# SBUF tiles in four pools by their role on TensorE, and a new plan for the same instructions

## The chip, the cores and the metric

One core of a Trainium2 chip runs the whole kernel. The metric is the device time of one execution in microseconds (us); lower is better. The profile names the engines PE (TensorE matmuls), PEld (TensorE weight loads, which overlap the matmuls), DVE (VectorE), ACT (ScalarE), POOL (GpSimd) and SP (the queue that starts nearly all DMAs).

## The reference

Attention by random features on 8 batches x 8 heads x 576 tokens x 64 columns, followed by a gated block on the 4608 x 512 result. All of it is float32.

```python
proj = einsum('bhsd,md->bhsm', x, omega); h = proj - sum(x*x)/2; phi = exp(h - max(h)) / sqrt(m)
kv = einsum('bhsm,bhsd->bhmd', k_p, v);  z = sum(k_p, axis=2)
attn = einsum('bhsm,bhmd->bhsd', q_p, kv) / (einsum('bhsm,bhm->bhs', q_p, z)[..., None] + 1e-06)
x = attn.transpose(0, 2, 1, 3).reshape(4608, 512)
out = ((x @ w_a) * (x @ w_b)) @ w_out          # 512 -> 1536 -> 512
```

## The kernel before

**Two kinds of work on PE.** The attention part consists of short float32 matmuls in bursts: projections (`four`, L633), the product of k features and v (`kv_burst`, L910), and the numerator (`num`, L982 and L985). The gated block consists of long matmuls in the rounded float32 type. Each float32 operand is split into a high and a low part, and a product is the sum of three matmuls (high-high, high-low, low-high). Of tokens there are 8 main blocks of 512 (b = 0 to 7), and one tail block (b = 8) that is made up of the last 64 tokens of each batch.

**The gated block.** `moe_block` (b = 0, 1) makes a and b with matmuls of 512 columns (L1319: stationary tile `w` or `u`, moving tile `x`, `Sa` or `Sb`) and multiplies the product with w_out by matmuls of 512 columns (`Out.mm`, L1129: stationary `ghl`, moving `wo`, three matmuls at a time). `moe_block7` (b = 2 to 8) uses a scheme with seven half-size products in place of eight. Its function `product` (L1405, matmuls at L1410) issues six matmuls of 256 columns, two moving tiles times three high-low combinations. One `unit` has seven products and one unit is one step; a main block has 12 steps. The stationary tile of a product is a slice of `w`, of `t` (reloaded from DRAM in every unit) or of `bq`; the moving tile is `x`, `Sa` or `Sb`. The products with w_out are again L1129 for b = 2 to 6, and for b = 7 and 8 a seven-product scheme at L1198 (stationary `ghl` or `og`, moving `wo` or `ot`). The results are added up from PSUM by DVE (L1420 and others).

**SBUF.** Every tile belongs to a ring of slots (L397 to L400); a slot is one tag in a tile pool, as large as its largest tile. Some tiles are guests in the slots of other rings (`IN_U` at L402, `LATE` at L405). For example `t` lives in u2 to u6, `bq` in a0 and a1, `xa` (first half of two of the four x tiles of a block) in xa0, xa1, u10 or u11, `ot` in X0, X1, hq1 and qd0, `og` in nat0, nat1, ht0 and ht1, and late `wo` tiles in hk0 and hq0 besides their own three slots. Constants come first and end at byte 1088 of each partition. Then one pool `sp` holds all other slots (L387, `alloc` at L409), which lie one behind another in the order in which the program first uses them. Slots for matmul operands are multiples of 512 bytes; between them lie small ones: `sm` with 192 bytes, `sq` with 64, `dn` with 36, `rd` with 20 (starts are rounded up to 32 bytes). So the starts of large tiles fall on all multiples of 32 modulo 256. In the built program, for example, both slots of `Sb` start at 128 modulo 256 (bytes 126848 and 164224), and the five slots in which `t` lives start at 160, 128, 128, 0 and 192 modulo 256 (bytes 25248, 156032, 160128, 181248, 204992). Below, the distance of a matmul is the byte address of its moving operand less that of its stationary operand, modulo 256. Slices within a tile start at multiples of 512 bytes, so the distance is the same for all slices.

**The plan.** All work is first written down as a graph of operations (class `Graph`). `schedule` then plays it through with a cost for each operation, a due time from `dues`, and a shift or tilt from the tables `SHIFT` and `TILT` (by number of the operation). That settles the order on each engine, whether a copy goes to ACT or to DVE, and which slot each tile gets. `PLACE` says at which step of the gated block the burst of each head pair u is put. In the last rows of the table, `CFG["XL"]` gives the steps of block 7 from which the tail block's x may be loaded (`xl`, first number) and split into high and low parts and sums (second number; L1525, L1526, `split` and `sums` with L424, L432 and L589). `CFG["LOWP"]` names raw weight pieces whose low part POOL extracts.

Of the kernel before, what the change touches and what calls it, by code (L numbers as in the profile page):

```python
# [15 lines left out]
X = mybir.AxisListType.X  # L16
# [3 lines left out]
B, H, S, D, M = 8, 8, 576, 64, 128  # L20
# [16 lines left out]
EPS = 1e-6 * M  # L37
KS = NHP

CFG = dict(TWIN=(0, 1, 2, 3, 4, 6, 7), LOWP=(1, 6, 10, 12, 13, 16, 19, 20, 21, 22, 25, 33, 34), SQP=('natk_0_0', 'natk_0_1', 'natq_0_0', 'natq_0_1', 'natq_0_3'), BW=365.0, DLAT=(1500, 2600), QUEUE=8, XL=(0, 2), JOIN=(6, 7, 8, 9, 10), LOWD=430, SQB=1, GLUE=700, TURNS=99, EDF=("DVE", "ACT", "POOL"), ROUNDS=1, SQUEEZE=1, CAP=("DVE", "ACT", "POOL"), ZS=600, ZB=(1500, 3000, 5000), ZD=(1500, 3000, 4500), HQ=(2500, 4000, 5000), BACK2=(1500, 2500, 4000), TW=(), WAIT=0, RAW=2000, FAST=(0, 1, 2, 3), JOIN0=False, WARM=8, HROOM=["w0", "u1", "w1", "u2", "w2", "u3"], H=3, TURN=(7,), BACK=1500, AT=2, MERGED=(5, 12, 13, 14, 15, 16, 17, 18, 19, 20, 21, 22, 23, 24, 25, 26, 27, 28, 29, 30, 31), SQPE=4, MARGIN=1200, LOAD=2500, SUMS=1400, NATS=(2,), CONV=(22000, 2200))  # L40


PLACE = {4: 3, 5: 4, 6: 7, 7: 9, 8: 10, 9: 12, 10: 14, 11: 18, 12: 20, 13: 21, 14: 27, 15: 29, 16: 33, 17: 35, 18: 38, 19: 41, 20: 45, 21: 47, 22: 50, 23: 54,
         24: 58, 25: 59, 26: 62, 27: 66, 28: 67, 29: 70, 30: 74, 31: 77, 32: 78, 33: 83}


SHIFT = {49: -8000, 89: 1500, 99: -4000, 123: 500, 156: -4000, 179: -1000, 253: 9500, 459: -1000, 558: -2000, 629: 500, 633: -500, 646: -4000, 730: 8000, 749:
         8000, 989: 4500, 995: -8000, 1081: 4000, 1200: 8000, 1207: 4000, 1339: 4000, 1352: 5000, 1483: -8000, 1546: 8000, 1587: 3000, 1957: -8000, 2016:
         1500, 2248: -2000, 2395: -8000, 2854: 3500, 3508: -4000, 3860: -2000, 3940: 6000, 4192: 2000}
TILT = {15: 800, 19: -800, 21: 800, 30: 3000, 34: -800, 58: 3000, 75: -3000, 79: 800, 81: 800, 88: -3000, 105: 800, 109: -800, 115: -3000, 124: 3000, 135:  # L50
# [9 lines left out]


class Buf:
# [7 lines left out]
    def part(self, k):  # L70
        return self, k
# [26 lines left out]
class Graph:  # L98
# [79 lines left out]
    def dues(self):  # L178
# [16 lines left out]
        for o in self.order:  # L195
            if "PE" in o.eng:
                idle += max(0, o.start - at - 5) * CFG["SQUEEZE"]
                at = o.end
# [11 lines left out]
        while heap:  # L210
            d, _, o = heapq.heappop(heap)
            e = next(iter(o.eng))
            cost = o.end - o.start if o.bytes else o.eng[e]
            if e in CFG["CAP"]:
                now = min(-d, ptr.get(e, inf))
# [12 lines left out]
    def plan(self):  # L228

        self.schedule()  # L230
        for _ in range(CFG["ROUNDS"]):
            self.dues()
            self.schedule()
        for o in self.ops:
            o.shift, o.tilt = SHIFT.get(o.n, 0), TILT.get(o.n, 0)
        self.schedule()
# [9 lines left out]
    def schedule(self):  # L246
# [12 lines left out]
        def entry(o, x, t):  # L259

            t = max(t, free[x] + 112 * (x == "DVE" and o.port == twice == 2))
            if x == "DVE" and o.port and port["POOL"][0] < t:
                t = max(t, port["POOL"][1] - 135)
            elif x == "POOL" and port["DVE"][0] <= t:
                t = max(t, port["DVE"][1] - 140)
            return t
# [20 lines left out]
        while len(done) < len(self.ops):  # L287
            best = None
            for e in engines:
                mine = None  # L290
                for o in ready[e]:
# [3 lines left out]
                    s = entry(o, e, max(o.need, at[0] + 92 * (e == "PE" and at[0] > 0)))  # L295
                    if o.bytes and len(landed) >= CFG["QUEUE"]:
                        s = max(s, landed[-CFG["QUEUE"]] + 100)
                    for x in o.eng:
# [3 lines left out]
                    else:  # L302


                        wait = CFG["WAIT"] if e == "DVE" and 0 <= o.prio < 4000 else 0
                        pr = o.shift + (o.prio if o.due is None or e not in CFG["EDF"] else o.due)
# [76 lines left out]
def tile_attention_moe(ctx: ExitStack, tc: tile.TileContext, kqt, kqtt, kqn, kqnt, vx, omst, idn, wab, wout, out):  # L383
    nc = tc.nc
    SQPE = CFG["SQPE"]
    const = ctx.enter_context(tc.tile_pool(name="const", bufs=1))
    sp = ctx.enter_context(tc.tile_pool(name="sp", bufs=1))  # L387
    ps = ctx.enter_context(tc.tile_pool(name="ps", bufs=1, space=PSUM))
    dram = ctx.enter_context(tc.tile_pool(name="dram", bufs=1, space=bass.MemoryType.DRAM))
    wide = wab.dtype == I64  # L390
# [6 lines left out]
    for name, n in dict(X=2, Xw=0, nat=2, x2=0, v=1, xg=1, hk=1, hq=3, qd=1, kvz=0, sm=3, sq=3, ht=3, Xt=1, xl=0, xts=2, rd=2, x=4, xa=2, xf=2, Sa=2, Sb=2, st=0,  # L397
                        w=NF // 2, rw=0, u=NF, t=0, tst=0, wo=3, raw=2, a=2, c=0, bq=0, ghl=2, osb=0, ot=0, owr=0, og=0, ogf=0, oc=0, zs=1, z2=1, zb=2, k2=4, dn=1, tails=0, zq=2, zx=2,
# [7 lines left out]
                oc=["v0", "xg0", "Xt0", "raw0", "raw1"])  # L406
    PS = {"at", "ab", "o"}

    def alloc(b):  # L409
        pool = ps if b.ring in PS else sp  # L410
        b.ap = pool.tile(b.shape, b.dtype, tag=b.slot, name=b.name)

    def fixed(shape, dtype, name):
# [27 lines left out]
    for k in range(4):  # L441
        g.op({"POOL": 110}, lambda e, k=k: nc.gpsimd.memset(ind.ap[D * (k // 2):D * (k // 2) + D, D * (k % 2):D * (k % 2) + D], SQ2 * (k in (0, 3))),
             w=[(ind, k)], alloc=[ind] if k == 0 else [], prio=-5000)
# [55 lines left out]
    for kind, i, ws in units:  # L499
        n = place[kind, i, ws[0]]  # L500
# [1005 lines left out]
    def bursts(step, place, banks):  # L1506

        for u, at in PLACE.items():
            if at == step:
# [25 lines left out]
    with tc.manual_schedule():  # L1535
        for o in order:
            for b in o.alloc:
                alloc(b)
            o.fn(next(iter(o.eng)))
# [74 lines left out]
```

## Time and profile before

| | us |
|---|---|
| median of three runs | 1033.49 (1033.02 to 1034.39) |
| profiled execution | 1033.61 |
| its span in the trace | 1031.8 |
| first matmul, last matmul's end (from the span's start) | 1.0, 1026.9 |

The profiled execution is 0.1 us above the median, and 1.8 us of its time lie outside of the span. "Busy" of an engine is the time in which at least one of its instructions runs. Matmuls are pipelined: one of 256 columns is listed with some 281 ns, but the next one starts some 118 ns after it. So what a stream of matmuls costs is read from the distance of starts, not from durations.

### The profile page before, as it was taken

The numbers are of one execution on the slowest core, as the hardware profiler recorded it, in microseconds if no ns is written. First come the engines' busy times: TensorE is split into PE (matmuls) and PEld (weight loads), VectorE is DVE, ScalarE is ACT, GpSimd is POOL, SyncE is SP. The second block draws the span as 40 slices with busy tenths as digits, with TensorE's granted clock in tenths as the row PEclk, the third lists the DMA queues.
The fourth block names the chain that finished last, engine by engine and source line by source line (L and its number), as shares of the span: only waits on it lengthen the run. The fifth ranks groups of instructions, "written<-read, shape, count | busy, mean of one in ns | idle before, by whom it ended". The sixth has DMA issues, their size and how long they took to land.

```text
span 1031.8 us, 27457 instructions
## 1 busy us (share of the span) xinstructions
PE 1021.0 (99%) x10538; PEld 902.8 (87%) x10538; DVE 876.7 (85%) x2162; ACT 575.5 (56%) x1584; POOL 109.1 (11%) x157
## 2 busy tenths in 40 slices
PE   9999999999999999999999999999999999999998
PEld 7777777777798989989998988988998999999998
DVE  6999999899997979877996889888877578999776
ACT  7998897667755647655663566475454024232221
POOL 0221222101111111111110111111110000000000
PEclk9999999999999999999999999999999999999999
DMA  9778877998899988999899989988887889999991
GB/s 353 292 254 258 283 247 244 309 327 303 297 318 375 323 293 296 339 307 298 276 314 339 301 272 321 334 261 299 280 297 251 279 297 332 307 348 334 366 322 43
DMA packets 123428, 306.76 MB, mean 297 GB/s; under 512 B 17952, under 2 KB 41248, under 8 KB 123296
## 3 DMA queue, kind: packets, MB, share of 16 engines
q1 hardware_dynamic: 122416, 304.34, 86.1%
q8 instruction: 83, 1.36, 0.5%
q10 hardware_dynamic: 880, 0.66, 0.2%
q14 instruction: 49, 0.40, 0.1%
HBM read 249.60 MB, written 55.34 MB: 296 GB/s over the span
## 4 chain that ended last, share of the span: by engine, by line
PE 91%; DVE 6%; ACT 2%; issue 1%; DVEq 0%; ACTq 0%
PE p L1410 40%; PE o L1129 23%; PE pb L1319 5%; PE pa L1319 5%; PE o_P L1198 5%; PE pkv L910 3%; PE ppk L633 3%; PE p L633 2%; PE p L982 2%; DVE sm L659 1%; DVE raw L482 1%; PE p L1198 1%; PE ppq L633 1%; PE pm L982 1%; ACT hk L672 0%
## 5 line engine op out<-in xcount | busy, mean ns | idle before, releaser
L1420 DVE TENSOR_TENSOR c<-p,c 128x512 f32<-128x512 f32 (+1 forms) x336 | 208.6, 621 | 72.1 <-PE p L1410 68.4
L1129 PE MATMUL o<-wo,ghl 128*128 128x512 f32 x1008 | 258.3, 397 | 0.0
L1129 PEld LDWEIGHTS o<-wo,ghl 128*128 128x128 f32 x1008 | 181.4, 188 | 39.7 <-issue 5.0
L1410 PE MATMUL p<-x,w 128*128 128x256 f32 x1008 | 136.5, 281 | 0.2
L1410 PEld LDWEIGHTS p<-x,w 128*128 128x128 f32 x1008 | 131.0, 188 | 6.5 <-DVE c L1420 0.6
L1410 PE MATMUL p<-Sa,t 128*128 128x256 f32 x1008 | 133.1, 281 | 0.0
L1410 PEld LDWEIGHTS p<-Sa,t 128*128 128x128 f32 x1008 | 125.5, 188 | 0.1
L424 ACT COPY c<-p 128x256 f32<-128x256 f32 x84 | 31.0, 369 | 121.6 <-PE p L1410 108.5
L940 ACT ACTIVATE hq<-hq,dn 128x128 f32<-128x128 f32 x224 | 69.7, 391 | 29.2 <-DVE dn L936 28.9
L857 POOL TENSOR_TENSOR z<-hk 128x256 f32<-128x256 f32 x28 | 24.4, 870 | 532.7 <-ACT hk L672 458.9
L1410 PE MATMUL p<-x,t 128*128 128x256 f32 x504 | 73.2, 281 | 0.8 <-DVE oc L1208 0.8
L1410 PE MATMUL p<-Sb,t 128*128 128x256 f32 x504 | 73.5, 282 | 0.0
L1410 PE MATMUL p<-Sb,bq 128*128 128x256 f32 x504 | 73.3, 281 | 0.0
L930 DVE CUSTOM_DVE_ANT_0 zero<-hq,zb 128x128 bf16<-128x128 f32 x224 | 68.8, 307 | 4.1
L672 ACT ACTIVATE hq<-hq,sm 128x128 f32<-128x128 f32 x196 | 64.8, 393 | 7.4 <-DVE sm L667 7.3
L1410 PEld LDWEIGHTS p<-x,t 128*128 128x128 f32 x504 | 66.1, 188 | 2.1 <-DVE oc L1208 1.0
L672 ACT ACTIVATE hk<-hk,sm 128x128 f32<-128x128 f32 x188 | 61.3, 393 | 8.2 <-DVE sm L667 8.1
L1410 PEld LDWEIGHTS p<-Sb,t 128*128 128x128 f32 x504 | 65.7, 189 | 0.0
L1410 PEld LDWEIGHTS p<-Sb,bq 128*128 128x128 f32 x504 | 65.5, 188 | 0.1
L432 DVE TENSOR_TENSOR ghl<-c,ghl 128x512 fp32r<-128x512 f32 (+1 forms) x86 | 54.2, 643 | 5.1 <-ACT ghl L424 4.5
L424 ACT CAST ghl<-c 128x512 fp32r<-128x512 f32 (+1 forms) x60 | 32.9, 566 | 45.8 <-PE o L1129 28.0
L1470 DVE TENSOR_TENSOR c<-c,c 128x512 f32<-128x512 f32 x82 | 55.5, 711 | 0.8
(245 smaller groups left out, 1903.6 us busy)
## 6 DMA issues: line engine op xcount, KB each, us to landing
t<-td SPq DMA_DIRECT2D x168, 512.0 KB
wo<-wod SPq DMA_DIRECT2D x96, 512.0 KB
bq<-bd SPq DMA_DIRECT2D x84, 256.0 KB
qdr<-qd SPq DMA_DIRECT2D x112, 144.0 KB
hq<-qdr SPq DMA_DIRECT2D x28, 576.0 KB
X<-in_kqt_dram SPq DMA_DIRECT2D x30, 512.0 KB
td<-ts SPq DMA_DIRECT2D x24, 512.0 KB
v<-in_vx_dram SPq DMA_DIRECT2D x28, 288.0 KB
```

The costliest lines, as they stand in the source:

```text
L424: nc.scalar.copy(o(), i())
L432: return lambda e: ENG[e].tensor_tensor(o(), i(), f(hi()), op=ALU.subtract)
L633: nc.tensor.matmul(flat4(pps[w])[half, c * M:c * M + M], x()[rows, c * P:c * P + P][:, half], om.ap[rows], start=True, stop=True)
L672: g.op({"ACT": 393 if b >= B1 or not own else 359}, lambda e, c=c, w=w, to=to, at=at: nc.scalar.activation(to.ap[:, at + c], src[w](c), AF ...
L930: g.op({"DVE": 302}, lambda e, c=c, qc=qc: nc.vector.tensor_tensor_reduce(out=junk.ap[:], in0=qc(), in1=zb.ap[:], scale=1.0, scalar=0.0, o ...
L940: g.op({"ACT": 392}, lambda e, c=c, src=src: nc.scalar.activation(hq.ap[:, c], src(), AF.Copy, scale=dn.ap[:, c:c + 1]), r=[sd, (dn, None) ...
L1129: nc.tensor.matmul(po.ap[:], ghl.ap[:, gi, t * P:(t + 1) * P], wo.ap[:, wi], start=(n == 0 and i == 0), stop=(n == NF - 1 and i == 2))
L1198: nc.tensor.matmul(pb.ap[:, t], A[0](ai)[:, t * P:(t + 1) * P], W[0](wi), start=begin and t == j == 0, stop=stop and t == 1 and j == 2)
L1319: nc.tensor.matmul(pb.ap[:], wt.ap[:, wi, c], xs[c].at(xi), start=(c == 0 and i == 0), stop=(c == NC4 - 1 and i == 2))
L1410: nc.tensor.matmul(pb.ap[:, half], wcol(wi, c), xc(xi, c), start=n == 0, stop=n == 5)
L1420: g.op({"DVE": dve(n)}, lambda e: nc.vector.tensor_tensor(c4.ap[:, o], pb.ap[:, half], y(), op=ALU.add), r=[*((pb, k) for k in range(half. ...
L1470: g.op({"DVE": dve(SM)}, lambda e, v=v, C=C: nc.vector.tensor_tensor(v(C[1]), v(C[1]), v(C[0]), op=ALU.mult), r=part, w=part[2:], prio=-10)
```

## The change

The instructions stay the same ones. The pool `sp` becomes four pools, opened one after the other. The first takes all slots that hold stationary operands and, with them, `wo`, which is moving in L1129 and L1198; the second takes only the slot sm0 (192 bytes); the third the slots with moving operands; the fourth all the rest. Besides, the tables of the plan are exchanged: `SHIFT` has some 170 entries in place of 32, `TILT` about as many as before with other entries, four bursts move in `PLACE` (15: step 29 to 30, 18: 38 to 40, 28: 67 to 68, 31: 77 to 76), `XL` goes from (0, 2) to (1, 3), and piece 22 leaves `LOWP` (there is no such piece: weight 7 is converted in one piece with number 21, since 7 is in `TWIN`).

```diff
-CFG = dict(TWIN=(0, 1, 2, 3, 4, 6, 7), LOWP=(1, 6, 10, 12, 13, 16, 19, 20, 21, 22, 25, 33, 34), ... XL=(0, 2), ...
+CFG = dict(TWIN=(0, 1, 2, 3, 4, 6, 7), LOWP=(1, 6, 10, 12, 13, 16, 19, 20, 21, 25, 33, 34), ... XL=(1, 3), ...
-PLACE = {4: 3, ... 15: 29, 16: 33, 17: 35, 18: 38, ... 28: 67, ... 31: 77, ...
+PLACE = {4: 3, ... 15: 30, 16: 33, 17: 35, 18: 40, ... 28: 68, ... 31: 76, ...
-SHIFT = {49: -8000, 89: 1500, 99: -4000, ...
+SHIFT = {14: 4000, 57: -1500, 70: 8000, 74: -3000, ...
-TILT = {15: 800, 19: -800, 21: 800, ...
+TILT = {11: -800, 13: 800, 15: 3000, ...
...
-    sp = ctx.enter_context(tc.tile_pool(name="sp", bufs=1))
+    sp = [ctx.enter_context(tc.tile_pool(name=f"sp{k}", bufs=1)) for k in range(4)]
...
+    STATIONARY, SHIM, MOVING = ("w", "u", "a", "ghl", "wo", "nat", "ht", "hk0", "hq0"), ("sm0",), ("x", "xa", "xf", "Sa", "Sb", "X", "qd", "hq1")
+
+    def part(slot):
+
+        names = (slot, slot.rstrip("0123456789"))
+        return next((k for k, part in enumerate((STATIONARY, SHIM, MOVING)) if any(n in part for n in names)), 3)
+
     def alloc(b):
-        pool = ps if b.ring in PS else sp
+        pool = ps if b.ring in PS else sp[part(b.slot)]
         b.ap = pool.tile(b.shape, b.dtype, tag=b.slot, name=b.name)
```

## Rows read from the trace of the kernel before

**Rows 1.** The page: busy time, share of the span, instructions of each engine.
```profile
PE 1021.0 (99%) x10538; PEld 902.8 (87%) x10538; DVE 876.7 (85%) x2162; ACT 575.5 (56%) x1584; POOL 109.1 (11%) x157
```

**Rows 2.** Stretch, length, busy us of PE, PEld, DVE, ACT, POOL; clock, DMA share, GB/s.
```profile
0.00:50.00 50.00, 47.38 (x732) 38.12 (x733) 41.81 (x106) 43.28 (x124) 5.66 (x14) 1.00 0.86 320
50.00:300.00 250.00, 247.75 (x2383) 194.68 (x2382) 238.27 (x618) 191.28 (x511) 44.75 (x58) 1.00 0.85 283
300.00:850.00 550.00, 550.00 (x5968) 495.96 (x5967) 445.45 (x1133) 290.77 (x834) 58.70 (x85) 1.00 0.90 303
850.00:870.00 20.00, 20.00 (x148) 18.93 (x147) 15.11 (x33) 7.65 (x17) 0.00 (x0) 1.00 0.93 346
870.00:930.00 60.00, 58.98 (x495) 58.37 (x494) 59.94 (x126) 21.03 (x46) 0.00 (x0) 1.00 0.94 326
```

**Rows 3.** Instruction groups of PE by line and shape: count, busy us, mean ns.
```profile
L1129 PE MATMUL o<-wo,ghl 128*128 128x512 f32 x1008 | 258.3, 397 | 0.0
L1410 PE MATMUL p<-Sa,t 128*128 128x256 f32 x1008 | 133.1, 281 | 0.0
L1410 PEld LDWEIGHTS p<-Sa,t 128*128 128x128 f32 x1008 | 125.5, 188 | 0.1
```

**Rows 4.** PE in order of time: products of Sb and t at distance 192.
```profile
294.03 0.86 PE L1410 MATMUL p<-Sb,t 128*128 128x256 f32 x6
294.73 0.50 PE L1410 MATMUL p<-x,t 128*128 128x256 f32 x3
...
992.01 0.87 PE L1410 MATMUL p<-Sb,t 128*128 128x256 f32 x6
992.71 0.86 PE L1198 MATMUL o_P<-ot,og 128*128 128x256 f32 x6
```

**Rows 5.** PE in order of time: product of Sb and t at distance 0, the last.
```profile
1000.48 0.88 PE L1410 MATMUL p<-Sb,t 128*128 128x256 f32 x6
1001.20 0.40 PE L1410 MATMUL p<-x,t 128*128 128x256 f32 x2
```

**Rows 6.** PE in order of time: products of Sb and t at distance 128.
```profile
309.50 0.88 PE L1410 MATMUL p<-Sb,t 128*128 128x256 f32 x6
310.22 0.64 PE L1410 MATMUL p<-x,t 128*128 128x256 f32 x4
...
355.24 0.89 PE L1410 MATMUL p<-Sb,t 128*128 128x256 f32 x6
355.97 0.40 PE L1410 MATMUL p<-x,t 128*128 128x256 f32 x2
...
1006.18 0.87 PE L1410 MATMUL p<-Sb,t 128*128 128x256 f32 x6
1006.89 0.64 PE L1198 MATMUL o_P<-ot,og 128*128 128x256 f32 x4
```

**Rows 7.** PE in order of time: twelve L1129 matmuls, at distance 192 and then 0.
```profile
236.17 2.96 PE L1129 MATMUL o<-wo,ghl 128*128 128x512 f32 x12
238.97 0.63 PE L1319 MATMUL pa<-x,wa 128*128 128x512 f32 x2
...
810.03 2.89 PE L1129 MATMUL o<-wo,ghl 128*128 128x512 f32 x12
812.76 0.40 PE L1410 MATMUL p<-x,w 128*128 128x256 f32 x2
```

**Rows 8.** Waits of PE: line, what it waited for, total us, times, longest us.
```profile
PE ppq L633 <- issue: 1.5, 1, 1.5
PE p L1410 <- DVE oc L1208: 0.8, 1, 0.8
```

**Rows 9.** Instructions with the tile xl: duration min/median/max ns, first and last start.
```profile
L435 SPq DMA_DIRECT2D xl<-xtd x4: 366/438/1942, 838.8 to 863.3; - x4
L432 DVE TENSOR_TENSOR x<-xl,x x4: 419/554/687, 854.2 to 877.7; 128x256 fp32r<-128x256 f32 x2, 128x512 fp32r<-128x512 f32 x2
L589 DVE TENSOR_TENSOR st<-xl,xl x2: 416/417/418, 853.2 to 877.3; 128x256 f32<-128x256 f32 x2
```

More of the change, by code (lines that the diff above doesn't have):

```diff
@@ L38 @@
 KS = NHP
-CFG = dict(TWIN=(0, 1, 2, 3, 4, 6, 7), LOWP=(1, 6, 10, 12, 13, 16, 19, 20, 21, 22, 25, 33, 34), SQP=('natk_0_0', 'natk_0_1', 'natq_0_0', 'natq_0_1', 'natq_0_3'), BW=365.0, DLAT=(1500, 2600), QUEUE=8, XL=(0, 2), JOIN=(6, 7, 8, 9, 10), LOWD=430, SQB=1, GLUE=700, TURNS=99, EDF=("DVE", "ACT", "POOL"), ROUNDS=1, SQUEEZE=1, CAP=("DVE", "ACT", "POOL"), ZS=600, ZB=(1500, 3000, 5000), ZD=(1500, 3000, 4500), HQ=(2500, 4000, 5000), BACK2=(1500, 2500, 4000), TW=(), WAIT=0, RAW=2000, FAST=(0, 1, 2, 3), JOIN0=False, WARM=8, HROOM=["w0", "u1", "w1", "u2", "w2", "u3"], H=3, TURN=(7,), BACK=1500, AT=2, MERGED=(5, 12, 13, 14, 15, 16, 17, 18, 19, 20, 21, 22, 23, 24, 25, 26, 27, 28, 29, 30, 31), SQPE=4, MARGIN=1200, LOAD=2500, SUMS=1400, NATS=(2,), CONV=(22000, 2200))
@@ L43 @@
[L43 to L49, printed above, removed]
@@ L50 @@
-TILT = {15: 800, 19: -800, 21: 800, 30: 3000, 34: -800, 58: 3000, 75: -3000, 79: 800, 81: 800, 88: -3000, 105: 800, 109: -800, 115: -3000, 124: 3000, 135:
[9 rows of a table removed]
+CFG = dict(TWIN=(0, 1, 2, 3, 4, 6, 7), LOWP=(1, 6, 10, 12, 13, 16, 19, 20, 21, 25, 33, 34), SQP=('natk_0_0', 'natk_0_1', 'natq_0_0', 'natq_0_1', 'natq_0_3'), BW=365.0, DLAT=(1500, 2600), QUEUE=8, XL=(1, 3), JOIN=(6, 7, 8, 9, 10), LOWD=430, SQB=1, GLUE=700, TURNS=99, EDF=("DVE", "ACT", "POOL"), ROUNDS=1, SQUEEZE=1, CAP=("DVE", "ACT", "POOL"), ZS=600, ZB=(1500, 3000, 5000), ZD=(1500, 3000, 4500), HQ=(2500, 4000, 5000), BACK2=(1500, 2500, 4000), TW=(), WAIT=0, RAW=2000, FAST=(0, 1, 2, 3), JOIN0=False, WARM=8, HROOM=["w0", "u1", "w1", "u2", "w2", "u3"], H=3, TURN=(7,), BACK=1500, AT=2, MERGED=(5, 12, 13, 14, 15, 16, 17, 18, 19, 20, 21, 22, 23, 24, 25, 26, 27, 28, 29, 30, 31), SQPE=4, MARGIN=1200, LOAD=2500, SUMS=1400, NATS=(2,), CONV=(22000, 2200))
@@ new lines @@
+PLACE = {4: 3, 5: 4, 6: 7, 7: 9, 8: 10, 9: 12, 10: 14, 11: 18, 12: 20, 13: 21, 14: 27, 15: 30, 16: 33, 17: 35, 18: 40, 19: 41, 20: 45, 21: 47, 22: 50, 23: 54,
+         24: 58, 25: 59, 26: 62, 27: 66, 28: 68, 29: 70, 30: 74, 31: 76, 32: 78, 33: 83}
+SHIFT = {14: 4000, 57: -1500, 70: 8000, 74: -3000, 76: 2000, 93: 8500, 106: 3000, 146: 7500, 178: 1500, 186: -7000, 188: -4000, 205: -14000, 207: -6000, 362:
[11 rows of a table added]
+TILT = {11: -800, 13: 800, 15: 3000, 26: 800, 28: 800, 34: 3000, 36: 3000, 43: 3000, 49: 3000, 58: -3000, 81: 800, 86: 3000, 94: 3000, 100: 3000, 109: 800,
[10 rows of a table added]
```

30 rows, old and new, of tables (SHIFT, TILT) are left out of this document.

## The prediction

> **What bounds the kernel now.** I read the busy times first, then the same by stretch, then the groups of PE, then PE in order of time. PE is busy for 1021.0 of 1031.8 us, DVE for 876.7 [rows 1]. [...] So only three things can move the time: the spacing of the matmuls, the few us in which PE stands still, and what lies before the first long matmul and after the last. DVE is close behind in places: 238.27 of 250 us, and 59.94 of the 60 us from 870 on [rows 2].
>
> Busy time doesn't show what a matmul costs. A 256-column matmul is listed with 281 ns [rows 3], while the six of one product fit into 0.70 to 0.73 us [rows 4, 6], the distance of two starts in the list by time. Over the 588 products of L1410 (3528 matmuls, of which one group stands in [rows 3]) the mean start-to-start is 118.3 ns (3521 spacings without a stall), 709.7 ns a product. Weight loads of 188 ns [rows 3] run under them.
>
> **This spacing depends on where the two operands lie.** The product of Sb and t is the clean case: same shapes, same line, same place in the step, and only the slot of t changes from step to step. At distance 192 the first and the last of 17 such products take 0.70 us (294.03 to 294.73, 992.01 to 992.71) [rows 4]; the mean of the 17 is 699.9 ns. At distance 0 the last of 33 takes 0.72 [rows 5], the mean is 716.2. At distance 128 the first, one in the middle and the last of 17 take 0.72, 0.73 and 0.71 [rows 6], the mean is 721.1. The order holds early and late, with POOL and ACT busy or idle, so it isn't the traffic of other engines. Other tiles agree: x and t at 192 702.4 (8 products), x and w at 192 697.5 (6), at 128 714.3 (6), at 0 713.3 (6). The 512-column matmuls of L1129 show another order: twelve at distance 192 take 2.80 us, twelve at distance 0 2.73 [rows 7]; over 9 and 5 such runs the means are 2.799 and 2.748, and by single spacings 233.4 ns at 192 (292), 232.1 at 128 (155), 230.7 at 64 (283), 230.2 at 0 (156), 231.8 over all.
>
> **The change part by part.** Pools: constants end at byte 1088, which is 64 modulo 256. The first new pool starts there, all its slots are multiples of 512 bytes, so every stationary slot and wo start at 64. Then 192 bytes of sm0, so every moving slot starts at 0 modulo 256. Moving less stationary is 192 for L1410 and L1319, and 0 for wo with ghl. I assume that pools lie in the order in which they are opened, without padding.
>
> (a) L1410, 3528 matmuls, is 588 products. One in seven uses the half tiles xa, and about half of these, 42, get u10 and u11, which are in the first pool: distance 0. The other 546 go from 709.7 to 700 ns, the mean of the 31 that lie at 192 in both halves: 546 x 9.7 ns = -5.3 us. The 42 at distance 0 cost 42 x 5 ns = +0.2 (between 713.3 and 716.2). Sum -5.1; with the ends 697.5 and 702.4, -6.5 to -3.8.
>
> (b) L1129, 1008 matmuls at distance 0: 1008 x (231.8 - 230.2) = -1.6 us; by the runs of twelve (229.0 each) -2.8.
>
> (c) L1319, 576 matmuls: mean 232.1, at 192 231.3 (42 spacings), -0.5 us, 0 to -0.9.
>
> (d) L1198, 510 matmuls (six of them begin at 992.71 [rows 4]): the 264 with ot lie at 192, 116.3 ns against 117.8 over all, -0.4; the 246 with wo at 0, 118.3, +0.1. Sum -0.3, between 0 and -0.6.
>
> (a) to (d) give -7.5 us, all of it on the path, since PE has no gap to hide it in. [...]
>
> (e) What DVE doesn't follow. From 870 to 930 DVE is full [rows 2]; a faster PE only waits there. This stretch is 60 of about 765 us of L1410, 0.4 us of (a); another 0.4 of (b) and (c) may go in the stretch to 300, where DVE is at 95%. Between 0 and +0.8; I take +0.4.
>
> (f) XL. The split of the tail block's x moves one step (7.8 us) later. On DVE it is eight L589 operations of 0.42 us, four L432 on x of 0.42 to 0.69 [rows 9] and four on Sa and Sb of 0.69: 8.4 us, about half of it before 870 and half at 877 to 882. The second half stands in the full queue where PE waited for DVE's L1208 for 0.8 us, at 876 [rows 8], within the 1.02 us that PE lacks there. If all that was done before 870 moves behind it, PE can lose 4.6 us; but from 850 to 870 DVE is free for 4.9 us [rows 2], and the first half still fits in the later part of it. So -1.0 to +4.6; I take -0.5, nearer to the end at which the stall goes, because the gate is a lower bound and not an order. The four xl loads on SP, issued from 838.8 to 863.3 [rows 9], move with it, past t, bq and wo loads of one step; the tail block starts only at about 930, so they and the casts on ACT cost nothing.
>
> (g) The tables. They redistribute PE's stops: 2.25 us to 300 [rows 2], of which 1.5 us is one wait of a projection for its bank [rows 8], and 2.6 us before 50 [rows 2]. The best that an order can do is to remove all 4.9; the worst is new stops of the size of those that are there. -4.9 to +3; I take -1.0, about the one large wait less something new. The four moved bursts carry their copies on ACT and DVE and their DMAs on SP along; they keep at least five steps (39 us) between a head pair's burst and the step that needs its result, as others do now: nothing. LOWP: no such piece, nothing. Short float32 matmuls: nothing, no row shows a dependence.
>
> Sum: -7.5 + 0.4 - 0.5 - 1.0 = -8.6. The profiled execution took 1033.6, 0.1 above the median: 1025.0 us.
>
> **The rivals.** First, DVE takes part of it back: (e) at +0.8 and (f) at +4.6, (g) at -0.5: 1033.6 - 7.5 + 0.8 + 4.6 - 0.5 = 1031.0. For it speaks that DVE is full for 60 us just there; against it the 4.9 us of room before. Second, placement itself does nothing, and the distance only stands for something else (which step, which neighbour in the queue): (f) and (g) remain, 1032.1. Against it speaks that the same product repeats 0.70 and 0.72 by slot through 700 us of the trace. Third, slower: the distance comes out wrong. The 192 bytes of sm0 set it alone. If between the pools lie another 192 bytes or 64 fewer, modulo 256, all of L1410 lies at 128: 546 x (721.1 - 709.7) = +6.2, with (b) -1.6 and (f), (g) -1.5: +3.1, 1036.7 us. The sign turns where a product costs more than 709.7 ns, so already at distance 0 (716.2: +3.5 in place of -5.3) little is left: 1033.6 + 3.5 - 3.3 = 1033.8. Against it: starts are rounded to 32 bytes now, and 192 is a multiple of that.
>
> **How the numbers follow.** My forecast has 0.74, DVE taking part of it 0.10, no effect of placement 0.09, a wrong distance 0.07. The forecast's own range comes from the ends: the low ends of (a) to (d) and half of (g) give 1020.5, the high ends of (a) to (d) with (f) and (g) at a small loss 1030. The first rival lies at 1031.0, so 1020.5 to 1031.0 leaves about 2 in 10 out: most of the other two rivals and the forecast's tails. A measurement of this kernel tells about 0.2% (2.1 us) from no change, which is 1031.4. Faster by more: the forecast, six tenths of the first rival and half of the second, 0.84; within 0.2%: the rest of these and part of the third, 0.09; slower: most of the third, 0.07.
>
> **What would show it.** In the profile after, six L1410 matmuls should take 0.70 us from start to start in nearly every product, with none at 0.72 or 0.73 except those with xa; twelve L1129 2.73 to 2.76. Seven products in a row should fall from 4.97 (7 x 709.7 ns) to 4.90 us. If the spacing falls and the time doesn't, PE's waits for DVE between 850 and 930 must have grown by as much. If the spacing stays at 709.7 in the mean, (a) to (d) are wrong. If PE's gaps to 300 and at 876 have gone, (f) and (g) are right; if new ones stand there, they are wrong.

## The result, and the profile of the changed kernel

| | kernel before | changed kernel |
|---|---|---|
| median (lowest to highest), us | 1033.94 (1033.02 to 1036.25) | 1025.27 (1024.35 to 1026.03) |
| ratio to before, 95% interval | 1 | 0.9912 (0.9893 to 0.9932) |
| profiled execution / its span, us | 1033.6 / 1031.8 | 1024.35 / 1022.5 |

The forecast was 1025.0 us. The total came out by luck: the terms for the spacing were too small in sum, the terms for PE's stops too hopeful, and the errors cancel. Medians, here and below, are of the fast runs: two slow ones, 3495 us of the kernel before and 5651 us of the kernel in which no step starts at distance 0, are left out. All lines of code move by 17: L1410 is L1427, L1129 is L1146, L1319 is L1336, L1198 is L1215, L633 is L650. The matmuls on each line are as many as before.

The page of the changed kernel and the windows by stretch, which answer to [rows 1, 2] (columns as there):

```profile
PE 1010.2 (99%) x10538; PEld 893.9 (87%) x10538; DVE 879.9 (86%) x2165; ACT 569.8 (56%) x1581; POOL 109.2 (11%) x157
```

```profile
0.00:50.00 50.00, 45.99 (x731) 37.09 (x732) 41.38 (x105) 43.79 (x125) 6.62 (x14) 1.00 0.85 321
50.00:300.00 250.00, 248.78 (x2394) 195.88 (x2393) 236.93 (x607) 194.58 (x522) 43.85 (x58) 1.00 0.85 284
300.00:850.00 550.00, 548.73 (x6002) 495.93 (x6001) 457.69 (x1162) 283.78 (x824) 58.72 (x85) 1.00 0.90 306
850.00:870.00 20.00, 19.17 (x146) 17.93 (x145) 14.64 (x29) 7.71 (x16) 0.00 (x0) 1.00 0.96 317
870.00:930.00 60.00, 60.00 (x516) 59.77 (x515) 59.97 (x127) 20.66 (x47) 0.00 (x0) 1.00 0.94 328
```

PE is still busy for all but 12 us. The gain lies in what it gets through: from 300 to 850 us it starts 6002 matmuls, 5968 before, although it now lacks 1.27 us there and lacked nothing. The clock is 1.00 in both. From 870 to 930 its busy time has no gap any more, with DVE as full as before; the starts show short stops there all the same (step (e) below).

The instruction groups (count, busy us, mean ns), for [rows 3]:

```profile
L1146 PE MATMUL o<-wo,ghl 128*128 128x512 f32 x1008 | 255.7, 395 | 0.0
L1427 PE MATMUL p<-Sa,t 128*128 128x256 f32 x1008 | 130.3, 278 | 0.0
L1427 PEld LDWEIGHTS p<-Sa,t 128*128 128x128 f32 x1008 | 122.6, 188 | 0.2 <-ACT c L441 0.2
```

The listed duration hides the change (281 to 278 ns); weight loads stay at 188 ns. So I go by starts again. Worked out from the spacings without a stall, times the count of matmuls (the rows of the trace give the starts; which tile lies where comes from the built program):

| | before: ns, total us | after: ns, total us | difference, us | predicted, us |
|---|---|---|---|---|
| L1410, 3528 matmuls | 118.3, 417.3 | 116.0, 409.1 | -8.2 | (a) -5.1 |
| L1129, 1008 | 231.8, 233.7 | 228.6, 230.5 | -3.2 | (b) -1.6 |
| L1319, 576 | 232.1, 133.7 | 233.3, 134.4 | +0.7 | (c) -0.5 |
| L1198, 510 | 117.8, 60.1 | 116.7, 59.5 | -0.6 | (d) -0.3 |
| sum | 844.7 | 833.4 | -11.3 | -7.5 |

The last matmul starts at 1017.25 us, 1026.65 before: 9.4 earlier. So 1.9 of the 11.3 us went to stops and to what lies between the long matmuls. The time in which no matmul runs between the first and the last grew from 4.9 to 6.3 us.

PE in order of time (start, us until the end of the group's last, line, tiles, count), two steps of seven products each (a group of twelve is two products); this is the view of [rows 4 to 7]:

```profile
305.35 1.58 PE L1427 MATMUL p<-x,w 128*128 128x256 f32 x12
306.76 1.58 PE L1427 MATMUL p<-Sa,t 128*128 128x256 f32 x12
308.18 0.87 PE L1427 MATMUL p<-Sb,t 128*128 128x256 f32 x6
308.88 0.87 PE L1427 MATMUL p<-x,t 128*128 128x256 f32 x6
309.59 0.87 PE L1427 MATMUL p<-Sb,bq 128*128 128x256 f32 x6
310.30 1.52 PE L1146 MATMUL o<-wo,ghl 128*128 128x512 f32 x6
...
395.25 2.90 PE L1146 MATMUL o<-wo,ghl 128*128 128x512 f32 x12
397.99 1.57 PE L1427 MATMUL p<-x,w 128*128 128x256 f32 x12
399.40 1.52 PE L1427 MATMUL p<-Sa,t 128*128 128x256 f32 x12
400.76 0.84 PE L1427 MATMUL p<-Sb,t 128*128 128x256 f32 x6
401.44 0.84 PE L1427 MATMUL p<-x,t 128*128 128x256 f32 x6
402.12 0.84 PE L1427 MATMUL p<-Sb,bq 128*128 128x256 f32 x6
402.80 1.54 PE L1146 MATMUL o<-wo,ghl 128*128 128x512 f32 x6
```

The first step takes 4.95 us, 0.70 to 0.71 for each product. The second takes 4.81, with Sb and t at 0.68, though these products all lie at distance 192 in both. What differs is the first product: in the second step its xa stands in u10 and u11, at distance 0. Twelve L1146 matmuls take 2.74 us (395.25 to 397.99), the 2.73 of distance 0 in [rows 7].

PE's waits (line, what it waited for, total us, times, longest), for [rows 8]:

```profile
PE pab L650 <- DVE a L1344: 1.2, 1, 1.2
PE ps L665 <- ACT x L659: 1.1, 1, 1.1
PE p L999 <- DVE ghl L449: 1.1, 1, 1.1
PE ppq L650 <- ACT qT L441: 1.0, 1, 1.0
PE p L1427 <- ACT oc L441: 0.7, 1, 0.7
```

The 1.5 us wait of L633 is gone. A wait for oc is there again, of nearly the old size, but in another place (855.2 us, two steps earlier in the program) and for ACT in place of DVE. The waits of 1.2 and 1.1 us are not among those of before; the one of L999, at 636.7 us, is most of what PE now lacks from 300 to 850. The tile xl, for [rows 9]:

```profile
L452 SPq DMA_DIRECT2D xl<-xtd x4: 434/524/600, 836.7 to 860.8; - x4
L449 DVE TENSOR_TENSOR x<-xl,x x4: 415/544/693, 859.0 to 897.8; 128x512 fp32r<-128x512 f32 x2, 128x256 fp32r<-128x256 f32 x2
L606 DVE TENSOR_TENSOR st<-xl,xl x2: 411/414/417, 857.5 to 888.8; 128x256 f32<-128x256 f32 x2
```

The first half of the split still runs before 870 us, the second some 12 to 20 us later than it did.

### The profile page after: what moved, and what is told of

It reads as the page before. It is cut to its first block, busy times and chain, and to the rows that moved or that the text cites. A ratio compares the mean times of both kernels' runs of the same rounds, so it can differ in the third digit from the quotient of the medians.

```text
span 1022.5 us, 27440 instructions
## 1 busy us (share of the span) xinstructions
PE 1010.2 (99%) x10538; PEld 893.9 (87%) x10538; DVE 879.9 (86%) x2165; ACT 569.8 (56%) x1581; POOL 109.2 (11%) x157
## 4 chain that ended last, share of the span: by engine, by line
PE 90%; DVE 6%; DMA 2%; ACT 1%; issue 0%; SPq 0%; DVEq 0%; ACTq 0%
PE p L1427 39%; PE o L1146 22%; PE pa L1336 6%; PE pb L1336 6%; PE o_P L1215 5%; PE ppk L650 2%; PE pkv L927 2%; PE p L650 2%; PE p L999 2%; PE p L1215 1%; DMA hq<-qdr 1%; DVE sm L676 1%; DMA X<-in_kqt_dram 1%; PE ppq L650 1%; DVE raw L499 1%; PE pm L999 1%
## 5 line engine op out<-in xcount | busy, mean ns | idle before, releaser
L1437 DVE TENSOR_TENSOR c<-p,c 128x512 f32<-128x512 f32 (+1 forms) x336 | 207.2, 617 | 60.1 <-PE p L1427 56.7
L1146 PE MATMUL o<-wo,ghl 128*128 128x512 f32 x1008 | 255.7, 395 | 0.0
L1146 PEld LDWEIGHTS o<-wo,ghl 128*128 128x128 f32 x1008 | 180.6, 188 | 37.4 <-issue 5.2
L1427 PE MATMUL p<-x,w 128*128 128x256 f32 x1008 | 135.7, 280 | 0.1
L1427 PEld LDWEIGHTS p<-x,w 128*128 128x128 f32 x1008 | 130.5, 189 | 6.2 <-DVE c L1437 0.7
L1427 PE MATMUL p<-Sa,t 128*128 128x256 f32 x1008 | 130.3, 278 | 0.0
L1427 PEld LDWEIGHTS p<-Sa,t 128*128 128x128 f32 x1008 | 122.6, 188 | 0.2 <-ACT c L441 0.2
L947 DVE CUSTOM_DVE_ANT_0 zero<-hq,zb 128x128 bf16<-128x128 f32 x224 | 72.6, 324 | 4.8
L1427 PE MATMUL p<-x,t 128*128 128x256 f32 x504 | 73.1, 281 | 0.9 <-ACT oc L441 0.7
L1427 PE MATMUL p<-Sb,bq 128*128 128x256 f32 x504 | 72.0, 279 | 0.0
L1427 PE MATMUL p<-Sb,t 128*128 128x256 f32 x504 | 71.8, 278 | 0.0
L1427 PEld LDWEIGHTS p<-x,t 128*128 128x128 f32 x504 | 65.6, 188 | 2.8 <-ACT oc L441 0.9
L1427 PEld LDWEIGHTS p<-Sb,bq 128*128 128x128 f32 x504 | 64.6, 188 | 0.1
L1427 PEld LDWEIGHTS p<-Sb,t 128*128 128x128 f32 x504 | 64.3, 188 | 0.0
L874 POOL TENSOR_TENSOR z<-z,hk 128x256 f32<-128x256 f32 x56 | 47.0, 838 | 66.3 <-ACT hk L689 63.5
```

The source lines that it names most:

```text
L874: g.op({"POOL": pool2(n)}, lambda e: nc.gpsimd.tensor_tensor(o(), a(), c(), op=ALU.add), r=r, w=w, alloc=list(al), prio=pri, deps=zload[-1 ...
L947: g.op({"DVE": 302}, lambda e, c=c, qc=qc: nc.vector.tensor_tensor_reduce(out=junk.ap[:], in0=qc(), in1=zb.ap[:], scale=1.0, scalar=0.0, o ...
L1146: nc.tensor.matmul(po.ap[:], ghl.ap[:, gi, t * P:(t + 1) * P], wo.ap[:, wi], start=(n == 0 and i == 0), stop=(n == NF - 1 and i == 2))
L1427: nc.tensor.matmul(pb.ap[:, half], wcol(wi, c), xc(xi, c), start=n == 0, stop=n == 5)
L1437: g.op({"DVE": dve(n)}, lambda e: nc.vector.tensor_tensor(c4.ap[:, o], pb.ap[:, half], y(), op=ALU.add), r=[*((pb, k) for k in range(half. ...
```

## The experiments

Two theories stood at the start: the pools make the gain (placement), or the new plan does. Later the two spacings seen above became a question of their own. The kernel before took 1034.1, 1034.25 and 1033.7 us beside the three sets of runs. All times are medians.

**Pools alone, on the old plan** (the change without XL, tables, places and LOWP):

```diff
-    sp = ctx.enter_context(tc.tile_pool(name="sp", bufs=1))
+    sp = [ctx.enter_context(tc.tile_pool(name=f"sp{k}", bufs=1)) for k in range(4)]
...
-        pool = ps if b.ring in PS else sp
+        pool = ps if b.ring in PS else sp[part(b.slot)]
```

> The plan of before, with the four pools. Placement theory: the spacing of the long matmuls falls as in the changed kernel (L1410 from 118.3 to 116.0 ns, L1129 from 231.8 to 228.6; 11.3 us in all by the starts in the two traces), and the new plan, which had 1.9 us more of stops and switches, is not there: 1033.9 - 11.3 = 1022.6 us, so faster than the changed kernel. Plan theory (the order of the work made the gain, the spacing only goes with it): 1033.9 us.

1024.24 us, ratio 0.9914 (0.9893 to 0.9935). The pools alone give the whole gain; the further 1.9 us that were expected from doing without the new plan are not to be seen. (The profiled execution of this kernel was granted 0.948 of the clock, so its rows are not read; the same kernel stands below once more.)

**The plan alone, in one pool** (the changed kernel with the two lines above put back and `part` taken out; its `SHIFT` has 146 entries in place of 33, its `TILT` 137 in place of 118):

> The new plan with all tiles in one pool. Placement theory: the spacings go back to 118.3 and 231.8 ns, and what is left is the plan's own 1.9 us of additional stops: 1035.8 us. Plan theory: 1025.3 us as the changed kernel.

1033.29 us, 0.9997 (0.9986 to 1.0008); L1410 is back at 118.25 ns, L1129 at 231.6. Waits of PE in it (L643 is L633, L1420 is L1410):

```profile
PE pab L643 <- DVE a L1337: 1.2, 1, 1.2
PE ps L658 <- ACT x L652: 1.1, 1, 1.1
PE p L1420 <- ACT oc L434: 0.7, 1, 0.7
```

These are waits of the changed kernel that before did not have, with the same sizes. The one of pab belongs to the plan: no run with the old plan has it. The one of ps doesn't, for the pools on the old plan (run again below) show it too:

```profile
PE ps L655 <- ACT x L649: 1.3, 1, 1.3
```

The plan removes stops and brings others, and is worth -0.3 us (-1.4 to +0.8); the 1.9 us of loss that were expected lie outside of this.

**The shim set to distance 0** (first added line), then **to 128** (second), on the changed kernel; the order of the instructions on each engine is the same in the built programs, since the planner doesn't see addresses:

```diff
-    STATIONARY, SHIM, MOVING = ("w", "u", "a", "ghl", "wo", "nat", "ht", "hk0", "hq0"), ("sm0",), ("x", "xa", "xf", "Sa", "Sb", "X", "qd", "hq1")
+    STATIONARY, SHIM, MOVING = ("w", "u", "a", "ghl", "wo", "nat", "ht", "hk0", "hq0"), (), ("x", "xa", "xf", "Sa", "Sb", "X", "qd", "hq1")
...
+    STATIONARY, SHIM, MOVING = ("w", "u", "a", "ghl", "wo", "nat", "ht", "hk0", "hq0"), ("zx0",), ("x", "xa", "xf", "Sa", "Sb", "X", "qd", "hq1")
```

> The changed kernel without the slot between the pools, so that moving and stationary operands of L1410 lie at distance 0 in place of 192, with the same order of instructions. Placement theory, by the kernel before's products at distance 0: 716 ns a product in place of 696, 588 x 20 ns = +12 us, about 1037. Plan theory: 1025.3, no change.

> The changed kernel with a slot of 128 bytes (zx0) between the pools in place of 192, distance 128. Placement theory, by the kernel before's products at 128: 721 ns, 546 x 25 ns = +14 us, about 1039; this is the wrong distance of the slower rival. Plan theory: 1025.3, no change.

At 0: 1037.31 us, 1.0031 (1.002 to 1.0042); L1410 119.8 ns, 718.6 for a product in the mean. At 128: 1035.94, 1.0017 (1.0008 to 1.0026); 119.1 ns, products of 715. So 192 bytes between two pools are worth 12 us, and the sign turns with them, as the third rival had it; 128 costs less than the 721 ns per product that Sb and t had shown in the kernel before. L1319 goes the other way from L1410. Twelve of its matmuls in the kernel at distance 0:

```profile
281.60 2.88 PE L1336 MATMUL pa<-x,wa 128*128 128x512 f32 x12
284.32 2.88 PE L1336 MATMUL pb<-x,wb 128*128 128x512 f32 x12
```

and the same in the changed kernel, at 192:

```profile
281.68 2.96 PE L1336 MATMUL pa<-x,wa 128*128 128x512 f32 x12
284.48 2.96 PE L1336 MATMUL pb<-x,wb 128*128 128x512 f32 x12
```

2.72 us against 2.80; over all 228.2 ns at 0, 232.6 at 128, 233.3 at 192.

A rival is left in these runs: with four pools all stationary slots start at 64 modulo 256, so the address of the moving operand alone would explain them as well as the distance. The kernel before tells the two apart. There all products of Sb and t have their moving operand at 128 modulo 256, and still they differ with the distance, as the prediction lists them (716.2 ns at 0, 721.1 at 128, 699.9 at 192); L1129 with wo at 0 modulo 256 takes 231.3 ns at distance 64 (145) and 233.0 at 192 (161).

**Distance 64** (another slot as the shim, `("sq0",)`):

> The changed kernel with a slot of 64 bytes in place of the 192 bytes of sm0 in the second pool: L1410, L1319 and half of L1198 come to distance 64. By the kernel before 256-column matmuls take 117.6 ns at 64 (117.1 at 192) and L1319 231.1 (231.2). If 64 behaves as it did there: L1410 3528 x (117.6 - 116.0) = +5.6 us, L1319 -1.3, 1029.6. If the shorter spacing of 113.3 ns is open to 64 as well: about 1025.

1031.1 us, 0.9966 (0.9953 to 0.9979). L1410 takes 117.8 ns at 64, a product 707 with hardly any spread (705 to 712), none near 680, also where the step starts at distance 0. L1319 takes 229.7.

**wo in the moving pool**, so that L1129 comes from 0 to 192:

```diff
-    STATIONARY, SHIM, MOVING = ("w", "u", "a", "ghl", "wo", "nat", "ht", "hk0", "hq0"), ("sm0",), ("x", "xa", "xf", "Sa", "Sb", "X", "qd", "hq1")
+    STATIONARY, SHIM, MOVING = ("w", "u", "a", "ghl", "nat", "ht", "hk0", "hq0"), ("sm0",), ("x", "xa", "wo", "xf", "Sa", "Sb", "X", "qd", "hq1")
```

> The changed kernel with wo in the moving pool: the 1008 matmuls of L1129 come from distance 0 to 192. Placement theory: by the kernel before 233.4 ns at 192 against 230.2 at 0, +3.2 us, and from the 228.6 that the changed kernel shows +4.8 us: 1028.5 to 1030.1. Rival, L1129 got faster for another reason than its distance (its neighbours, the plan): 1025.3, 228.6 ns stays.

1026.58 us, 0.9925 (0.9912 to 0.9938). Twelve of its matmuls:

```profile
398.36 2.96 PE L1146 MATMUL o<-wo,ghl 128*128 128x512 f32 x12
401.16 1.57 PE L1427 MATMUL p<-x,w 128*128 128x256 f32 x12
```

2.80 us again; over all 232.9 ns, +4.3 us, as placement said. But the time rose by 1.3 us only, because L1410 fell from 409.1 to 406.4 us: 332 of 560 products were short (690 ns or less), 231 of 566 in the changed kernel. That was in neither expectation, and the time lies below both of them.

**What chooses between 707 and 680 ns.** In the changed kernel the 36 steps that start at distance 0 take 712, 700, 682, 683, 682, 690 and 688 ns, 4837 in sum; the 48 others 699 each, 4895. Two runs move only the slots of xa.

All 84 steps start at 0:

```diff
-    STATIONARY, SHIM, MOVING = ("w", "u", "a", "ghl", "wo", "nat", "ht", "hk0", "hq0"), ("sm0",), ("x", "xa", "xf", "Sa", "Sb", "X", "qd", "hq1")
+    STATIONARY, SHIM, MOVING = ("w", "xa", "u", "a", "ghl", "wo", "nat", "ht", "hk0", "hq0"), ("sm0",), ("x", "xf", "Sa", "Sb", "X", "qd", "hq1")
```

> The changed kernel with the slots of xa in the first pool too, so that the first product of all 84 steps of L1410 lies at distance 0 (in the changed kernel 36 do). Theory A, a long product at distance 0 leaves the products behind it in the shorter of two spacings: by the trace of the changed kernel the seven products of a step take 4837 ns where the first lies at 0 (712, 700, then 682 to 690) and 4895 where it lies at 192 (699 each), so 48 steps x 58 ns = -2.8 us: 1022.5. Theory B, each product takes what its own distance gives: 48 x (712 - 696) ns = +0.8 us: 1026.0. In the trace A wants about 682 ns for the third to fifth product of every step, B 692 in the mean with both spacings.

No step does (u10 and u11 in the moving pool):

```diff
-    STATIONARY, SHIM, MOVING = ("w", "u", "a", "ghl", "wo", "nat", "ht", "hk0", "hq0"), ("sm0",), ("x", "xa", "xf", "Sa", "Sb", "X", "qd", "hq1")
+    STATIONARY, SHIM, MOVING = ("w", "u", "a", "ghl", "wo", "nat", "ht", "hk0", "hq0"), ("sm0",), ("x", "xa", "u10", "u11", "xf", "Sa", "Sb", "X", "qd", "hq1")
...
-        names = (slot, slot.rstrip("0123456789"))
+        names = (slot, slot.rstrip("0123456789") if slot not in ("u10", "u11") else slot)
```

> The reverse: u10 and u11 in the moving pool, so that no product of L1410 lies at distance 0 (48 matmuls of the 512-column projections come to 0 by it, some 0.2 us). Theory A: 36 x 58 ns = +2.1 us, 1027.4, and up to 1031.9 if no step falls into the shorter spacing (84 steps of 7 x 707 ns). Theory B: 36 x (712 - 696) ns = -0.6 us, 1024.7. In the trace A wants hardly any product of 680 ns, B as many as before.

All: 1024.08 us, 0.9899 (0.9886 to 0.9911); the third to fifth product of a step take 682 to 683 ns over all 84 steps, L1410 405.7 us (-3.4). None: 1026.58 us, 0.9924 (0.9912 to 0.9937); the products take 697 to 700 ns, L1410 410.5 us (+1.4). Theory A holds in the trace, at nearly the size that it gave for the first (-2.8) and two thirds of the second (+2.1). In the time it is not shown by these two alone: 0.9899 and 0.9924 lie on the right sides of the changed kernel's 0.9912, but the intervals overlap. The last set of runs tells more. The step of 397.99 us above, in the kernel where its first product lies at 192:

```profile
398.55 1.58 PE L1427 MATMUL p<-x,w 128*128 128x256 f32 x12
399.96 1.58 PE L1427 MATMUL p<-Sa,t 128*128 128x256 f32 x12
401.37 0.87 PE L1427 MATMUL p<-Sb,t 128*128 128x256 f32 x6
402.08 0.87 PE L1427 MATMUL p<-x,t 128*128 128x256 f32 x6
402.79 0.87 PE L1427 MATMUL p<-Sb,bq 128*128 128x256 f32 x6
403.49 1.52 PE L1146 MATMUL o<-wo,ghl 128*128 128x512 f32 x6
```

4.94 us where it had been 4.81: the same matmuls on the same instruction order, one tile moved. Distance 0 is not the only thing that brings the short spacing: 177 of 564 products have it here without any.

**The late split alone** (the kernel before with `XL=(1, 3)`):

> The kernel before with XL=(1, 3) alone, the later split of the tail block's x. By the step (f) of the prediction -0.5 us (-1.0 to +4.6): 1033.7 beside 1034.2. If it were worth the whole 1.0 us of the stop at 876 us, 1033.2; if DVE's full queue takes it, 1038.8. In the trace: DVE's eight sums of x before 870 us go behind it, and the wait of PE at 876 us (0.8 us) is gone or not.

1034.09 us, 1.0006 (0.9997 to 1.0016): no gain, and at most 1.7 us of loss. Two products of x and t in the kernel before, two steps apart, and the same two here:

```profile
862.76 0.86 PE L1410 MATMUL p<-x,t 128*128 128x256 f32 x6
876.80 0.97 PE L1410 MATMUL p<-x,t 128*128 128x256 f32 x6 [0.78 <-DVE oc L1208]
```

```profile
862.81 0.98 PE L1410 MATMUL p<-x,t 128*128 128x256 f32 x6 [0.67 <-ACT oc L424]
877.48 0.87 PE L1410 MATMUL p<-x,t 128*128 128x256 f32 x6
```

The stop at 876 us went, as the prediction said, and one of nearly the same size came two steps earlier, where PE now waits for ACT's copy to oc. Every trace with the late split has it there, and every trace without has the old one: it goes with the split.

**Three kernels side by side**: the pools on the old plan again, the same with xa in the first pool, and the changed kernel again.

> The kernel before with the four pools once more, for a trace at the full clock. If the plan is worth nothing, it takes what the changed kernel takes, within 1 us (1024 to 1026), with L1410 at 116.0, L1129 at 228.6 and L1319 at 233.3 ns. If the plan's sum of -1.5 us is real, 1.5 us more than the changed kernel: 1026.8.

> The kernel before with the four pools and xa in the first of them: the old plan, and the first product of all 84 steps at distance 0. Theory A (a product at distance 0 brings the shorter spacing): L1410 in some 405.7 us as in the run where all steps start at 0, 3.4 us less than in the changed kernel, so 1.5 to 3.4 us below the run of the pools on the old plan that goes beside it: about 1022. If the plan and not the spacing had set that run's time: the same as the pools on the old plan, 1024.2.

> The changed kernel once more, beside the two before it: 1025.3 again, L1410 116.0 ns in the mean, 36 of 84 steps with the shorter spacing.

| | median (range), us | ratio to before | L1410, us | short products |
|---|---|---|---|---|
| pools, old plan | 1024.74 (1023.42 to 1027.10) | 0.9920 (0.9908 to 0.9933) | 408.7 | 250 of 568 |
| changed kernel | 1024.26 (1023.98 to 1025.06) | 0.9915 (0.9901 to 0.9928) | 408.8 | 245 of 566 |
| pools, old plan, all steps at 0 | 1022.24 (1021.15 to 1022.81) | 0.9893 (0.9879 to 0.9906) | 406.0 | 342 of 566 |

The old and the new plan take the same time within what this tells. The third kernel is the fastest here; every run of it is below every run of the other two. Its 2.7 us less on L1410 than the first are as much as the 2.5 us between their medians; the two traced executions lie only 1.1 us apart, since one wait takes 1.2 us back there (below). Its page:

```profile
PE 1008.8 (99%) x10538; PEld 891.1 (87%) x10538; DVE 875.4 (86%) x2162; ACT 575.6 (56%) x1584; POOL 110.8 (11%) x157
```

One wait of [rows 8] in the third and then in the first kernel, which share the order of the kernel before (L640 is L633):

```profile
PE ppq L640 <- issue: 1.4, 1, 1.4
```

```profile
PE ppq L640 <- issue: 0.2, 1, 0.2
```

1.5 us in the kernel before, 1.4 and 0.2 here: it varies where the plan is the same. The row names no releaser; that it waits for its bank, as the prediction had it, is not shown.

## Why the prediction was right, step by step

**That placement moves the time** was right, and so was the layout: the pools alone 0.9914 and 0.9920, the plan alone 0.9997, and 192 bytes of shim decide the sign. The second rival (placement does nothing) falls with the same runs. The third had the sign right, with 128 a little too dear (1036.7 us said, 1035.9 measured) and 0 too cheap (1033.8 said, 1037.3 measured; the 3.3 us that it takes off there are 0.2 more than its (b), (f) and (g) give).

**(a)** was too small: -8.2, outside -6.5 to -3.8. The step that failed is to give every product the price of its own distance, "700 ns, the mean of the 31 that lie at 192", whatever stands before it. Those 31 stood in the kernel before between products at other distances, where short ones hardly occur: 5 of 581. In the changed kernel the 48 steps that start at 192 take 699 ns a product, as said. The 36 that start at 0 were said to take 713 + 6 x 700 = 4913 ns and took 4837; 36 x 76 ns = 2.7 of the 3.1 us that were missing. The prediction counted 42 such products and booked them as a loss of 0.2 us. What stands behind them was the best part.

**(b)** was too small: -3.2 against -1.6. The prediction had both prices, 230.2 ns by single spacings and 229.0 by runs of twelve (-2.8), and took the first. That wo and ghl all lie at 0 is not enough for 228.6 ns: they do so too where L1410 lies at 0, 64 or 128, and there L1129 takes 229.9, 230.2 and 230.0 ns, the price that was taken. The difference is in the first six matmuls of each run of L1129: 229.5 ns in the mean in the changed kernel, 231.3 to 231.6 in those three. From the seventh on it is 227.1 to 227.9 in all four. So here too the step that failed is to price a matmul by its own distance, without the stream before it. With wo at 192, 232.9 ns (233.4 in the kernel before) shows what its own distance does.

**(c)** had the wrong sign: +0.7 where -0.5 was said and nothing above zero was allowed for. The 231.3 ns at 192 came from 42 spacings; over 526 it is 233.3. L1129's 512-column matmuls had already shown the order 0, 64, 128, 192 from fast to slow in 886 spacings, and L1319 follows just that (228.2, 229.7, 232.6, 233.3 ns). The nearest row was the other line with the same shape, not the few spacings of the same line.

**(d)** -0.6 against -0.3, at its end.

**(e)** came out at about its size (+0.4), though busy time, 60.00 of 60 us from 870 to 930, hides it. By starts, six matmuls of 256 columns in that stretch are followed by the next only after 179 to 222 ns, 0.5 us more than at 117 ns each; in the second trace of the changed kernel six are again, also 0.5 us. The same instructions in one pool, or with the shim at 0, 64 or 128, where PE is slower, have none above 150 ns there. Each time PE goes on 0.05 to 0.1 us after an operation of DVE on c or oc has ended, as here after the one that starts at 898.45 and lasts 0.68:

```profile
898.45 0.68 DVE L1225 TENSOR_TENSOR oc<-p,oc 128x512 f32<-128x512 f32 x1
899.18 0.97 PE L1427 MATMUL p<-x,t 128*128 128x256 f32 x6
```

The first rival, whose 4.6 us hung on that stretch, falls: the late split alone costs at most 1.7 us.

**(f) and (g)**, together -1.5 us, were worth nothing that can be measured: -0.3 (-1.4 to +0.8) for the whole plan in one pool, -0.5 between the two plans in four pools, +0.4 for the late split alone. Two steps failed. Moving the split did remove the wait at 876 us, but nothing was set against it for what the new order brings: 0.7 us two steps earlier. And the 1.5 us wait at 251.6 us was taken as a property of the order, though the order that had it shows 0.2 us as well. What would show it was named rightly: new stops stand in place of the old.

The sum: 3.8 us more gain from spacing than said, 3.0 us less from the rest (-1.1 said for (e) to (g), +1.9 found in these two traces, and PE stands still for 6.3 us in one trace of the changed kernel and for 7.5 in the other, 4.9 before). A right total out of two wrong groups of terms is luck; the mechanism, spacing by placement, was right.

## What to carry to other kernels

Where matmuls run without a gap, list their start-to-start spacing by the distance of their operands' addresses, and place by it; but run a sweep of the distance for each shape, since of the four that were run the best for 256 columns (192: 116.0 ns on L1410, 117.8 to 119.8 at the others) was the worst for 512 (233.3 ns on L1319, 228.2 to 232.6). A price that is read where kinds are mixed need not give their cost when all become one kind (231.3 ns for L1319 at 192 before, 233.3 after): bound it by the longest unmixed run that there is. Look at what runs before a stream as well: the same matmuls at the same distance took 680 or 707 ns for six, by what stood before them. And credit a stop as removed only if it repeats from run to run, and look for the place to which the new order moves it.

## What the runs showed of the hardware that I had not expected

At distance 192 the 256-column matmuls of L1410 have two spacings, 113.3 ns (products of 680) and 117.8 (707), and few in between (41 of 534 products in the changed kernel lie between 690 and 705 ns). The short one, once there, stays: in the changed kernel none of the 167 short products with another product at 192 directly behind it was followed by a long one (stalls left aside). It can end where other matmuls stand between: after a stream of L1129 at distance 0 alone, the next product at 192 was long in all 43 cases, after one at distance 192 (the run with wo moving) in 23 of 40. It begins most often behind a product at distance 0 (there by the third product in 33 of the 36 steps that start so), and the single spacings show it coming: 120, 120, 120, 121, 122, 116, then 113 or 114 throughout. With L1410 at 0, 64 or 128 no product falls below 703 ns.

So what stands before a product matters as well as its own distance (680 or 707 ns at 192). Why PE keeps the one spacing or the other, no row shows; that stays open, and so does whether a distance that was not run (32, 96, 160, 224) does better; in the kernel before, these took 117.5, 119.2, 118.7 and 118.2 ns, beside 117.1 at 192. L1319 at 0 with L1410 at 192 would be worth some 2.9 us more by an estimate from these runs (576 x 5.1 ns), but both read x from the same slots; that was not tried.
